# Moving crossbar transposes behind the weight loads: PE transposes for twelve units instead of eight, in a fused attention and MLP kernel

## The chip, the cores and the metric

The kernel runs on one core of a Trainium2 chip. A core has TensorE (PE: matrix products and transposes into PSUM), VectorE (DVE), ScalarE (ACT), GpSimd (POOL) and SyncE (SP, which here only issues transfers), and 16 DMA engines that all of them share. The metric is device time in microseconds of a whole execution, the median of several runs. Times within an execution come from the hardware profiler and count from its first instruction.

## What is computed

Attention with a feature map of exponentials, over 8 batches and 8 heads (576 rows, 64 columns each), and behind it, on the joined heads, a normalization and a two-layer MLP with a residual:

```python
def phi(x):
    proj = einsum('bhsd,df->bhsf', x, w_phi)              # 64 -> 128 features
    proj = proj - max(abs(proj), axis=-1, keepdims=True)
    return concatenate([exp(proj), exp(-proj)], axis=-1)
q_p, k_p = phi(q), phi(k)
kv  = einsum('bhsf,bhsd->bhfd', k_p, v)
z   = sum(k_p, axis=2)
num = einsum('bhsf,bhfd->bhsd', q_p, kv)
den = einsum('bhsf,bhf->bhs', q_p, z)[..., None] + 1e-06
x = (num / den).transpose(0, 2, 1, 3).reshape(8, 576, 512)
# ... then, row by row of x:
xn  = (x - mean(x)) / sqrt(var(x) + 1e-06) * g_ln
out = x + maximum(xn @ w_ch1, 0) @ w_ch2                  # 512 -> 2048 -> 512
```

Inputs and output are float32. Products run in bf16.

## The kernel before

**Units and pairs.** The 64 heads are worked on two at a time: 32 *units*, numbered n, of two heads each (rows of two heads side by side make 128 partitions' worth of columns). Eight units make a *pair* of batches (4 pairs). When a pair's units are done, its rows x are normalized, transposed (tile xT) and go through the MLP in three rounds of 384 rows: `hT_ps` = first product, `hT` = relu, `ch_ps` = second product, `o` = result, stored.

**Order of work.** All operations are given to a list scheduler that runs in Python when the kernel is built. Each has a rank, guessed durations and dependencies; the scheduler plays them through and puts them into each engine's program in the order in which its model started them. The ranks are latest start times plus an offset per kind of operation (table `OFF`, one row for each of three stages of the kernel), found by tuning. Engines then run their programs strictly in order.

**q and k must be turned.** The feature product needs q and k with their 64 columns on the partitions. There are two ways. For units below QK_DMA, PE turns the upper halves of the float32 words (bf16 by truncation), 8 transposes for the rows in the main tiles and 1 for the mixed tile that holds the last rows, and VectorE or ScalarE copies them out of PSUM:

```python
X_DMA, QK_DMA = 1, 8
# ...
def a_trans(u):
    # ... main: into PSUM tile qkT_ps (8 transposes)
    nc.tensor.transpose(
        ps[:, (i * 4 + c) * P : (i * 4 + c + 1) * P],
        qkb[:, i, hh, 4 * c * D + 1 : 4 * (c + 1) * D : 2], ident,
    )
    # ... mixed: into PSUM tile qxT_ps (1 transpose)
    # then copies into u["qkT"]: ("DVE", "ACT"), modelled (0.6, 0.93) and (0.16, 0.22) us
```

For the rest, the tile is first cast to bf16 (on whichever of VectorE, ScalarE and GpSimd the scheduler picks), and one transfer on SyncE's queue turns all nine 128x128 tiles through the crossbar on its way from SBUF to SBUF:

```python
def a_trans_dma(u):
    # ... cast_mixed, cast_main: ("DVE", "ACT", "POOL")
    def turn():
        u["qkT"] = qkT_bufs[j]
        nc.sync.dma_start_transpose(
            out=u["qkT"].rearrange("p (c t) -> p c t", t=P), in_=b16
        )
    dma("SP", rank, 0, turn, r=[("b16x", n % 2), ("b16", n % 2)],
        w=[("qxT", j), ("qkT", j, 0), ...], us=1.2, tiles=72)
```

In pair 0 the PSUM tile of the main transposes comes from the small tiles' pool (`ps_B`, three buffers); from unit 8 on it would come from `ps_A`, two large buffers that the scores of k and q (`pm`), the tails (`pt`) and the numerators (`num`) use as well.

**After the turn**, per unit: `pm` = scores of k and of q (4 products each), their maxima on VectorE (`m`), exponentials on ScalarE (`eb`, and `ea` from `pt`), scaled v on GpSimd (`vv`), `KV` on PE and a copy, numerators `num` on PE, their scaling on VectorE (`numc`, `rden`), and the division into x on GpSimd.

**Weights.** w_phi is loaded twice, into both halves of the partitions, and cast into a block-diagonal `wbk`. g (`gln`) scales the normalized rows. w_ch1 and w_ch2 (4.2 MB each in float32) are cast on the way by GpSimd's queue in four pieces each:

```python
nc.scalar.dma_start(out=wphi_f[0:D, :], in_=w_phi)
nc.scalar.dma_start(out=wphi_f[D : 2 * D, :], in_=w_phi)
# ... casts into wbk on VectorE
def load_w1(n, V, gate):      # waits for an early q/k/v load to have come
def load_w2(n, V):            # four loads, after the last piece of w1 has come
    # ...
    dma("POOL", V, 1 << 20, emit, r=[("w1 came", NW - 1)], w=[("w2", n)], us=0.85)
```

**The filler.** Until the scheduler's time 45 (WARM), PE gets a product of zeros whenever it has nothing else, so that it doesn't fall idle (line L1215, 120 columns each).

**The first loads**, by queue:

```python
load_main("k", 0, 1, -4.0, "SP")
load_main("q", 0, 1, -4.0, "ACT")
load_tails("k", 0, -3.0, "SP")
load_tails("q", 0, -3.0, "ACT")
load_main("v", 0, 1, -2.8, "SP")
load_main("k", 1, 1, -2.6, "SP")
load_main("q", 1, 1, -2.6, "ACT")
load_tails("v", 0, -2.4, "SP")
load_weights()                # g, on ACT's queue
load_main("v", 1, 1, -1.0, "SP")
```

Of the kernel before, what the change touches and what calls it, by code (L numbers as in the profile page):

```python
# [17 lines left out]
def bcast(ap: bass.AP, dim: int, n: int) -> bass.AP:  # L18
# [2 lines left out]
    return dataclasses.replace(ap, ap=new_ap)  # L21


DUE = 24.7
BLOCK = 127.5
RELU = -983.1
WARM = 45.0
X_DMA, QK_DMA = 1, 8
GATE = (("k", 3), ("k", 3), ("v", 3), ("v", 3))
OFF = (  # L30
    {
        "load": 291.2, "trans": 434.7, "trans.copy": 59.4, "mixed": -235.7, "mixed.max": -33.4,
        "mixed.exp": 269.7, "k": -70.1, "k.max": 134.5, "k.em": -242.4, "k.exp": -244.7,
        "en": 2.0, "vv": -236.4, "q": 197.1, "q.max": 56.3, "q.em": 267.7, "tails": -434.9,
        "tails.exp": -54.1, "kv": -342.1, "kv.copy": 60.1, "num0": -115.0, "num1": -4.8,
        "num.dve": 25.8, "put": 44.8, "ln": 232.4, "w1": -144.2, "w2": 330.3,
    },
    {
        "load": -33.4, "trans": 205.3, "trans.copy": 224.5, "mixed": 13.2, "mixed.max": -126.5,
        "mixed.exp": -37.8, "k": -79.5, "k.max": 229.0, "k.em": -204.8, "k.exp": 170.4,  # L40
        "en": -210.7, "vv": 14.0, "q": 271.6, "q.max": 83.8, "q.em": -232.1, "tails": -412.8,
        "tails.exp": -43.8, "kv": 80.5, "kv.copy": 400.8, "num0": -204.4, "num1": -95.2,
        "num.dve": 30.7, "put": 84.9, "ln": 271.1, "w1": -341.2, "w2": -67.5,
    },
    {
        "load": 108.9, "trans": 8.9, "trans.copy": 96.2, "mixed": -247.8, "mixed.max": -231.2,
        "mixed.exp": 118.7, "k": -33.5, "k.max": 47.1, "k.em": 39.2, "k.exp": 9.3, "en": -174.0,
        "vv": -109.4, "q": -27.3, "q.max": 37.9, "q.em": 195.5, "tails": -210.6,
        "tails.exp": 417.3, "kv": 29.7, "kv.copy": 177.5, "num0": 79.5, "num1": 83.1,
        "num.dve": -26.3, "put": -25.4, "ln": 1.0, "w1": -277.0, "w2": 28.2,  # L50
    },
)

# [131 lines left out]
def kernel(  # L185
# [21 lines left out]
    nc = tc.nc  # L207
    P = 128

    B, H, S, D = q.shape  # L210
# [3 lines left out]
    KC = DM // P  # L214
# [7 lines left out]
    TG = 4  # L222
# [6 lines left out]
    NM = RN // P  # L229
    XB = 3  # L230
    QB = 3
    NW = 4
# [13 lines left out]


    wphi_f = consts.tile([P, F], FP32, name="wphi_f")
    nc.scalar.dma_start(out=wphi_f[0:D, :], in_=w_phi)
    nc.scalar.dma_start(out=wphi_f[D : 2 * D, :], in_=w_phi)  # L250
    gln_sb = consts.tile([P, KC], FP32, name="gln")
    ngln = consts.tile([P, KC], FP32, name="ngln")
# [58 lines left out]
    add = sched.add  # L311
# [4 lines left out]

    backlog = {"DMA": 0.0, "DMA_w": 0.0}

    def dma(queue, rank, nbytes, emit, r=(), w=(), us=0.6, lag=2.2, tiles=0, row=1024):


        key = ("dma", len(sched.ops))
        kind, other = ("DMA_w", "DMA") if queue == "POOL" else ("DMA", "DMA_w")
        ns = 0.094 if queue == "POOL" else 0.018 if row == 256 else 0.046
        packets = nbytes / (2048 if queue == "POOL" else row) / 16
        pieces = max(1, round(packets * ns / 1.2))

        def transfer(now, free):
            backlog[kind] -= packets / pieces
            if tiles:  # L330
                return tiles * 0.015
            both = free.get(other, 0.0) > now
            turn = 0.046 if queue == "POOL" else 0.094
            return packets * (ns + turn * both) / pieces

        def issued(now, free):
            both = free.get(other, 0.0) > now or backlog[other] > 0
            wait = max(0.0, free.get(kind, 0.0) - now) + backlog[kind] * (0.046 + 0.094 * both)
            backlog[kind] += packets
            return max(us, wait) if tiles else us  # L340


        add(queue, issued, rank, emit, r=r, w=(key, *w))
        for i in range(pieces):
            last = i == pieces - 1
            add(kind, transfer, rank, None, r=(key, *r) if last else (key,),
                w=(*w, key) if last else (key,), lag=lag if last else 0.0)

    def issue(queue, rank, dst, src, keys, nbytes, row=1024):
        eng = nc.sync if queue == "SP" else nc.scalar  # L350
        dma(queue, rank, nbytes, lambda: eng.dma_start(out=dst, in_=src), w=keys, row=row)

    def heads(pair, i, half):

# [36 lines left out]
    def load_tails(key, n, rank, queue):  # L391

        t = {"q": q, "k": k, "v": v}[key]
        pair, i = divmod(n, H)
        j = n // TG % 2
        for half in range(2):
            b, h, step = heads(pair, i, half)
            ps_ = slice(half * 64, half * 64 + 64)
            dst = vx_bufs[j][ps_, :, half, 0:D] if key == "v" else (
                qx_bufs[j][ps_, :, "qk".index(key), :]  # L400
            )
            src = bass.AP(
                tensor=t.tensor, offset=t.offset + ((b * H + h) * S + 4 * P) * D,
                ap=[[D, 64], [step * S * D, TG], [1, D]],
            )
            issue(queue, rank, dst, src, [(key + "x" + str(half), j)], 16384 * TG, row=256)

    def loaded(u, key):
        g, hh, j = u["g"], u["hh"], u["n"] // TG % 2
# [1 line left out]

    def load_weights():
        def gln():
            nc.scalar.dma_start(out=gln_sb, in_=moe_g_ln.rearrange("(kc p) -> p kc", p=P))

        dma("ACT", -1.5, 2048, gln, w=["gln"])
        add(
            "DVE", 0.1, (0.0,), lambda: nc.vector.tensor_scalar_mul(out=ngln, in0=gln_sb, scalar1=-1.0),
            r=["gln"], w=["ngln"],
        )  # L420
# [108 lines left out]
    def a_trans_dma(u):  # L529

        n = u["n"]
        j = n % QB
        b16 = b16_bufs[n % 2]

        def cast(engine, out, in_):
            if engine == "DVE":
                nc.vector.tensor_copy(out=out, in_=in_)
            elif engine == "ACT":
                nc.scalar.copy(out=out, in_=in_)
            else:  # L540
                nc.gpsimd.tensor_tensor(
                    out=out, in0=in_, op=ALU.mult,
                    in1=bcast(bcast(one[:, 0], 1, in_.shape[1]), 2, in_.shape[2]),
                )

        def cast_mixed(engine):
            cast(
                engine, b16[:, MX * P :].rearrange("p (i d) -> p i d", i=2),
                qx_bufs[n // TG % 2][:, n % TG, :, :],
            )  # L550

        def cast_main(engine):
            cast(
                engine, b16[:, 0 : MX * P].rearrange("p (i f) -> p i f", i=2),
                qk_bufs[u["g"] % NBUF][:, :, u["hh"], :],
# [8 lines that stand above are left out]
        rank = rk("trans", n)  # L564
        add(("DVE", "ACT", "POOL"), (0.12, 0.22, 0.4), rank, cast_mixed, r=[*loaded(u, "q"), *loaded(u, "k")],
            w=[("b16x", n % 2)])
        add(("DVE", "ACT", "POOL"), (0.6, 1.02, 2.1), rank, cast_main, r=[*loaded(u, "q"), *loaded(u, "k")],
            w=[("b16", n % 2)])
        dma("SP", rank, 0, turn, r=[("b16x", n % 2), ("b16", n % 2)],
            w=[("qxT", j), ("qkT", j, 0), ("qkT", j, 1), *[("T", j, i) for i in range(3)]], us=1.2, tiles=72)  # L570

    def a_mixed(u):

# [342 lines left out]
    def x_trans_dma(pr, r, V):  # L916
        xi, j = (pr["pair"] * NR + r) % len(xc_bufs), (pr["pair"] * NR + r) % XB

        def turn():
            nc.sync.dma_start_transpose(  # L920
                out=xT_bufs[j], in_=xc_bufs[xi].rearrange("p i f -> p (i f)")
            )

        dma("SP", V, 0, turn, r=[("xc", xi, i) for i in range(NM)],
            w=[("xT", j, kc) for kc in range(KC)], us=1.2, tiles=NM * KC * 8)

    def x_stats(pr, t, half, V):

# [169 lines left out]
    for pair in range(NPAIR):  # L1098
# [5 lines left out]
        for i in range(H):  # L1104
            n = pair * H + i
# [12 lines left out]

    moe_V = 1000.0
    add("POOL", 5.0, -9.0, None)  # L1120
    add("ACT", 1.8, -9.0, None)
    add("SP", 0.7, -9.0, None)
    add("DVE", 4.3, -9.0, None)
    add(
        "ACT", 1.3, -1.0,
        lambda: nc.scalar.preload_act_table_set("natural_log_exp_and_others"),
# [4 lines left out]
    load_tails("q", 0, -3.0, "ACT")  # L1131
    load_main("v", 0, 1, -2.8, "SP")
    load_main("k", 1, 1, -2.6, "SP")
    load_main("q", 1, 1, -2.6, "ACT")
    load_tails("v", 0, -2.4, "SP")
    load_weights()
    load_main("v", 1, 1, -1.0, "SP")
# [5 lines left out]
    for n in range(NU + 2):  # L1143
        m = n + 4
        if n % HG == 0 and m < NU:
            rank = rk("load", m)
# [31 lines left out]
        if n >= 1 and n <= NU:  # L1178
            w = units[n - 1]
            pr, i = pairs[w["pair"]], w["i"]  # L1180
            V = rk("ln", n - 1)
            tiles = range(NT)
            if w["pair"] == 0:
                tiles = range(4) if i < 4 else range(4, NT)
                half, i = i % 4 // 2 if i % 2 else None, i % 4 + 4 * (i == 7)
            else:
                half = i // 4 if i % 4 == 3 else None
# [65 lines left out]
```

## Time and profile before

| what | value |
|---|---|
| time, median of 3 runs | 390.57 us (389.93 to 390.85) |
| span of the profiled run | 388.8 us, mean granted PE clock 0.988 |
| packets and bytes | 92444 packets, 53.28 MB, mean 137 GB/s |
| crossbar transposes of q and k | 24 (units 8 to 31), median landing 3.2 to 5.3 us by tile |
| filler products | 22.4 us of PE's busy time |
| MLP first product, second product | 153.3 us and 145.3 us of PE's busy time |

The lines of the profile itself stand in the prediction, where each is read. A few things on reading them. In the page's 40 slices one slice is 9.72 us here; a digit is tenths of busy time, and on the clock's row tenths of full speed. In a timeline a row is a run of like instructions: start, duration, engine, line of the kernel, operation, output<-input, count, and in brackets how long the engine was idle before it and what ended that. SPq, ACTq and POOLq are sequencers that issue transfers; a transfer's end isn't in that row but in the answer's "DMA to landing". Products on PE are pipelined: a single row's duration includes the way through the array, so the pace of a group is its total over its count.

### The profile page before, as it was taken

How to read it: one execution, taken by the hardware profiler on the slowest of the kernel's cores; microseconds unless marked ns; L12 is line 12 of the kernel's file. 1: busy time of each engine (PE TensorE's matmuls, PEld its weight loads, DVE VectorE, ACT ScalarE, POOL GpSimd, SP SyncE). 2: the span in 40 equal slices, each digit the busy share in tenths (PEclk: the TensorE clock that was granted, in tenths of full speed). 3: DMA queues.
4: the chain of work that ended last, by engine and by line, in shares of the span. 5: the costliest groups of instructions: out<-in, count | busy, mean ns of one | idle time of the engine just before them, and what ended most of it. 6: DMA issues, size and time to landing. Idle time of an engine off the chain costs nothing.

```text
span 388.8 us, 8917 instructions
## 1 busy us (share of the span) xinstructions
PE 364.6 (94%) x3307; PEld 232.5 (60%) x3354; DVE 255.0 (66%) x556; ACT 259.8 (67%) x576; POOL 201.9 (52%) x348
## 2 busy tenths in 40 slices
PE   3999995999999989999999999999999999999993
PEld 1888864666766554666666556666665555555541
DVE  3788995899999999997897998696757000000000
ACT  2877885899786857797976887686946444444411
POOL 3667987577576836664936655935841111111022
PEclk9999998799999999999999999999999999999998
DMA  7999889979799284948861486220007030110012
GB/s 208 300 227 279 262 150 170 222 189 254 197 245 232 64 230 111 236 129 190 183 186 36 124 163 157 57 60 2 30 27 137 31 90 29 27 56 27 30 66 71
DMA packets 92444, 53.28 MB, mean 137 GB/s; under 512 B 58992, under 2 KB 87792, under 8 KB 92400
## 3 DMA queue, kind: packets, MB, share of 16 engines
q1 hardware_dynamic: 86400, 47.79, 48.8%
q0 software_dynamic: 4224, 4.19, 6.9%
q10 hardware_dynamic: 1776, 0.72, 0.7%
q8 instruction: 26, 0.43, 0.5%
q14 instruction: 18, 0.15, 0.1%
HBM read 36.77 MB, written 9.44 MB: 119 GB/s over the span
## 4 chain that ended last, share of the span: by engine, by line
PE 57%; issue 21%; DVE 11%; DMA 6%; POOL 3%; ACT 1%; POOLq 0%; SPq 0%; DVEq 0%
PE hT_ps L1006 20%; PE ch_ps L1037 16%; PE pm L624 6%; DMA qkT_130<-b_0_131 4%; PE n_bank L734 3%; POOL o L1056 3%; PE num L780 3%; PE n_bank L1215 2%; PE pt L699 2%; DVE m_137 L631 1%; DVE m_135 L631 1%; DMA qx_106<-in_k_dram 1%; DVE w_120 L451 1%; DVE st_147 L933 1%; PE n_bank L729 1%
## 5 line engine op out<-in xcount | busy, mean ns | idle before, releaser
L1037 PE MATMUL ch_ps<-w_121,hT 128*128 128x512 bf16 x541 | 145.3, 379 | 1.6
L1006 PEld LDWEIGHTS <-w_120 128*128 128x128 bf16 x768 | 72.7, 98 | 55.9 <-issue 2.5
L1016 ACT ACTIVATE hT<-hT_ps 128x384 bf16<-128x384 f32 x113 | 55.6, 493 | 59.4 <-PE hT_ps L1006 58.9
L1037 PEld LDWEIGHTS <-hT 128*128 128x128 bf16 x576 | 53.3, 98 | 43.8
L820 POOL TENSOR_TENSOR x<-numc,rden 128x384 bf16<-128x384 f32 (+3 forms) x88 | 46.2, 541 | 62.4 <-DVE rden L814 58.2
L1056 POOL TENSOR_TENSOR o<-o,x 128x512 f32<-128x512 f32 x26 | 30.1, 1157 | 85.9 <-ACT o L1050 80.5
L1006 PE MATMUL hT_ps<-xT_127,w_120 128*128 128x384 bf16 x256 | 52.0, 326 | 0.1
L1006 PE MATMUL hT_ps<-xT_125,w_120 128*128 128x384 bf16 x256 | 50.2, 329 | 1.4 <-DVE hT L1014 0.9
L1006 PE MATMUL hT_ps<-xT_126,w_120 128*128 128x384 bf16 x256 | 51.2, 326 | 0.1
L1014 DVE TENSOR_SCALAR hT<-hT_ps 128x384 bf16<-128x384 f32 x79 | 42.9, 549 | 9.8 <-PE hT_ps L1006 9.2
L643 ACT ACTIVATE eb_134<-pm 128x1024 bf16<-128x1024 f32 x32 | 32.8, 1036 | 3.5 <-DVE m_137 L631 1.5
L643 ACT ACTIVATE eb_133<-pm 128x1024 bf16<-128x1024 f32 x32 | 31.7, 1025 | 4.9 <-DVE m_137 L631 3.8
L705 ACT ACTIVATE ea_118<-pt 128x1024 bf16<-128x1024 f32 x32 | 31.9, 1032 | 4.0 <-PE pt L699 2.4
L705 ACT ACTIVATE ea_116<-pt 128x1024 bf16<-128x1024 f32 x32 | 31.5, 1028 | 4.2 <-PE num L786 1.5
L631 DVE TENSOR_REDUCE m_136<-pm 128x8 f32<-128x1024 f32 x22 | 26.6, 1215 | 6.4 <-PE pm L624 6.3
L631 DVE TENSOR_REDUCE m_135<-pm 128x8 f32<-128x1024 f32 x22 | 26.7, 1215 | 4.0 <-PE pm L624 4.0
L1045 DVE SCALAR_TENSOR_TENSOR o<-ch_ps,rstd_157,x 128x512 f32<-128x512 f32 x2 | 1.5, 752 | 41.4 <-PE ch_ps L1037 41.4
L631 DVE TENSOR_REDUCE m_137<-pm 128x8 f32<-128x1024 f32 x20 | 24.3, 1214 | 2.1 <-PE pm L624 2.1
L1215 PE MATMUL n_bank<-wz 128*128 128x120 bf16 x301 | 22.4, 221 | 1.6 <-DVE KV L742 1.0
L804 DVE TENSOR_TENSOR numc<-num,em 128x390 f32<-128x390 f32 (+1 forms) x40 | 20.3, 515 | 4.6 <-PE num L780 4.4
L810 DVE TENSOR_TENSOR numc<-numc,num 128x390 f32<-128x390 f32 (+1 forms) x40 | 20.4, 515 | 0.7
L1215 PEld LDWEIGHTS <-wz 128*128 128x128 bf16 x301 | 18.6, 101 | 3.1 <-issue 2.1
(204 smaller groups left out, 649.5 us busy)
## 6 DMA issues: line engine op xcount, KB each, us to landing
out_dram<-o SPq DMA_DIRECT2D x32, 256.0 KB, 2.5
qk_100<-in_k_dram SPq DMA_DIRECT2D x12, 256.0 KB, 3.8
v_101<-in_v_dram SPq DMA_DIRECT2D x12, 256.0 KB, 3.7
qk_102<-in_k_dram SPq DMA_DIRECT2D x10, 256.0 KB, 3.4
qk_102<-in_q_dram SPq DMA_DIRECT2D x10, 256.0 KB, 4.1
v_103<-in_v_dram SPq DMA_DIRECT2D x10, 256.0 KB, 4.6
qk_104<-in_k_dram SPq DMA_DIRECT2D x10, 256.0 KB, 4.0
qk_104<-in_q_dram SPq DMA_DIRECT2D x10, 256.0 KB, 4.7
```

What stands on the lines that cost most here:

```text
L624: nc.tensor.matmul(ps[:, 2 * c : 2 * c + 2, :], u["qkT"][:, (i * 4 + c) * P : (i * 4 + c + 1) * P], wbk, start=True, stop=True,)
L631: nc.vector.reduce_max(out=u["m"][:, i, 0:MX], in_=u["pm", i], axis=AX.X, apply_absolute_value=True)
L643: nc.scalar.activation(u["EB"][:, t, 0:MX, :], u["pm", 1], AF.Exp, scale=(1.0, -1.0)[t])
L705: nc.scalar.activation(u["EA"][:, t, 0:1024], u["pt"], AF.Exp, scale=(1.0, -1.0)[t])
L810: nc.vector.tensor_add(out=st["numc"], in0=st["numc"], in1=st["ps"][0])
L820: nc.gpsimd.tensor_tensor(out=dst, in0=st["numc"][ps_, i : i + n, 0:D], in1=bcast(st["rden"][ps_, i : i + n], 2, D), op=ALU.mult,)
L1006: nc.tensor.matmul(st["ps"], w1_sb[:, kc, jj * P : (jj + 1) * P], xT_bufs[(pair * NR + r) % XB][:, kc::KC, :], start=(kc == 0), stop=(kc = ...
L1014: nc.vector.tensor_relu(h_sb, st["ps"])
L1016: nc.scalar.activation(h_sb, st["ps"], AF.Relu)
L1037: nc.tensor.matmul(ch[t], hT[r, jj][:, rt * P : (rt + 1) * P], w2_sb[:, jj, :], start=(jj == 0), stop=(jj == JC - 1),)
L1056: nc.gpsimd.tensor_tensor(out=ch["o", t], in0=ch["o", t], in1=x[:, t, :], op=ALU.add)
L1215: nc.tensor.matmul(warm, wz, wz[:, 0:WN], start=False, stop=False, skip_group_check=True)
```

## The change

It has five parts.

- QK_DMA goes from 8 to 12: units 8 to 11, the first half of pair 1, are turned on PE instead of through the crossbar.
- The first crossbar transpose, now that of unit 12, waits for all four pieces of w_ch2.
- The two halves of w_phi go out on two queues, SyncE's and ScalarE's, instead of both on ScalarE's.
- The second unit's q and g move from ScalarE's queue to SyncE's.
- The scheduler's model of transfers changes (issue 0.5 us and landing 1.5 us instead of 0.6 and 2.2; a transpose keeps its queue for 1.29 us; the start of each engine is set anew), and the whole table of offsets is tuned again. This changes the order of work everywhere.

It is meant to keep crossbar transposes apart from the loads of the weights, and to start the first products sooner.

```diff
-DUE = 24.7
-BLOCK = 127.5
+DUE = 39.9
+BLOCK = 136.7
-X_DMA, QK_DMA = 1, 8
+X_DMA, QK_DMA = 1, 12
 OFF = (
     {
-        ... "ln": 232.4, "w1": -144.2, "w2": 330.3,
+        ... "ln": 323.9, "w1": -204.9, "w2": 513.0,
     },
     # ... (all entries of all three rows are new)
@@ w_phi
-    nc.scalar.dma_start(out=wphi_f[0:D, :], in_=w_phi)
+    nc.sync.dma_start(out=wphi_f[0:D, :], in_=w_phi)
     nc.scalar.dma_start(out=wphi_f[D : 2 * D, :], in_=w_phi)
@@ model of a transfer
-    def dma(queue, rank, nbytes, emit, r=(), w=(), us=0.6, lag=2.2, tiles=0, row=1024):
+    def dma(queue, rank, nbytes, emit, r=(), w=(), us=0.5, lag=1.5, tiles=0, row=1024):
-        pieces = max(1, round(packets * ns / 1.2))
+        pieces = 1 if tiles else max(1, round(packets * ns / 1.2))
             if tiles:
-                return tiles * 0.015
+                return 0.1
@@ g
-            nc.scalar.dma_start(out=gln_sb, in_=moe_g_ln.rearrange("(kc p) -> p kc", p=P))
-        dma("ACT", -1.5, 2048, gln, w=["gln"])
+            nc.sync.dma_start(out=gln_sb, in_=moe_g_ln.rearrange("(kc p) -> p kc", p=P))
+        dma("SP", 0.15, 2048, gln, w=["gln"])
@@ a_trans_dma
-        dma("SP", rank, 0, turn, r=[("b16x", n % 2), ("b16", n % 2)],
-            w=[("qxT", j), ("qkT", j, 0), ("qkT", j, 1), *[("T", j, i) for i in range(3)]], us=1.2, tiles=72)
+        dma("SP", rank, 0, turn, r=[("b16x", n % 2), ("b16", n % 2)]
+            + [("w2", i) for i in range(NW) if n == QK_DMA],
+            w=[("qxT", j), ("qkT", j, 0), ("qkT", j, 1), *[("T", j, i) for i in range(3)]], us=1.29, tiles=72)
@@ starts of the engines in the model, first loads
-    add("ACT", 1.8, -9.0, None)
-    add("SP", 0.7, -9.0, None)
-    add("DVE", 4.3, -9.0, None)
+    add("ACT", 1.3, -9.0, None)
+    add("SP", 1.3, -9.0, None)
+    add("DVE", 3.6, -9.0, None)
-    load_main("q", 1, 1, -2.6, "ACT")
+    load_main("q", 1, 1, -2.5, "SP")
```

## The prediction

> **What bounds the kernel now.** I first read the first two parts of the page, shares of engines and the span in 40 slices, because they say which engine could set the end and where it fails to.
>
> ```profile
> PE 364.6 (94%) x3307; PEld 232.5 (60%) x3354; DVE 255.0 (66%) x556; ACT 259.8 (67%) x576; POOL 201.9 (52%) x348
> PE   3999995999999989999999999999999999999993
> DVE  3788995899999999997897998696757000000000
> PEclk9999998799999999999999999999999999999998
> ```
>
> PE is busy 94% of the span. It has one dent in the middle (the 5 in the seventh slice, 58 to 68 us), and there its granted clock drops as well (8 and 7). But in the first 48 us "busy" isn't work: the kernel pads PE with products of zeros (the filler, L1215) to keep its clock. So I asked for busy time by stage: all instructions first, then those of L1215 alone, whose first row is the last line here. The columns are the stretch, its length, busy us and count of each engine, granted clock, DMA share, GB/s.
>
> ```profile
> 0.00:48.00 48.00, 39.52 (x613) 35.03 (x617) 35.43 (x83) 33.07 (x75) 31.32 (x74) 1.00 1.02 258
> 48.00:63.00 15.00, 14.00 (x179) 10.10 (x178) 14.03 (x30) 12.85 (x32) 12.92 (x24) 1.00 0.95 151
> 63.00:75.00 12.00, 7.79 (x63) 5.10 (x61) 6.85 (x16) 6.76 (x12) 6.05 (x15) 0.72 1.23 233
> 120.00:160.00 40.00, 37.52 (x305) 21.81 (x309) 38.72 (x85) 29.46 (x66) 25.42 (x37) 1.00 0.67 178
> 160.00:200.00 40.00, 39.68 (x397) 26.31 (x400) 35.17 (x70) 32.50 (x70) 24.09 (x41) 1.00 0.74 180
> ...
> 0.00:48.00 48.00, 22.18 (x299) 18.50 (x299) 1.00 1.02 258
> ```
>
> There are three regimes. **The head**, to 48 us: PE does 39.5 - 22.2 = 17.3 us of real work; VectorE, ScalarE and the transfers (share 1.02) set its pace. **The body**, from 48 us to the last product at about 382.5: there is no filler, and PE is the bound (39.68 of 40 us from 160 to 200). **The tail**, 6 us of last result, addition and store. In a body bound by PE each idle microsecond and each microsecond of slow clock moves the end one for one. From 120 to 160 PE idles 2.5 us, because VectorE is full (38.72 of 40). The other hole is 63 to 75, and the timeline shows whose it is (start, duration, engine, line; in brackets the idle time before and its releaser):
>
> ```profile
> 51.05 2.30 POOL L435 DMA_DIRECT2D w_121<-in_moe_w_ch_dram  x3
> 52.16 2.38 SPq L560 DMA_TRANSPOSE qkT_130<-b_0_131  x1
> 55.06 0.81 POOL L435 DMA_DIRECT2D w_121<-in_moe_w_ch_dram  x1
> 60.56 6.37 SPq L560 DMA_TRANSPOSE qkT_128<-b_1_132  x1
> 67.59 1.03 PE L624 MATMUL pm<-wbk,qkT_130 128*128 128x256 bf16 x4 [3.71 <-DMA qkT_130<-b_0_131]
> 67.76 0.69 DVE L537 CAST b_0_131<-qk_104 128x1024 bf16<-128x1024 f32 x1 [3.87 <-DMA qkT_130<-b_0_131]
> 67.62 0.30 ACT L539 CAST b_0_131<-qx_106 128x128 bf16<-128x128 f32 x1 [3.31 <-DMA qkT_130<-b_0_131]
> ```
>
> The first crossbar transpose (unit 8) is issued at 52.16, between the second weight matrix's loads (51.05 to 55.9), and lands at 67.54. PE, VectorE and ScalarE all end up waiting for it. The groups for its source and for the weight tile give the usual landing times, minimum, median and maximum:
>
> ```profile
> DMA to landing us min/median/max: 3.2/3.6/15.4
> DMA to landing us min/median/max: 8.8/13.6/15.9
> ```
>
> So the 15.4 us belong to one transpose, not to the operation: its median is 3.6, and 15.4 is the length of a weight load. The chain that ended last also runs through this transfer (4.0% of the span, its largest DMA share).
>
> **What the Trainium skill says.** "DMA: Bandwidth & Descriptors", section Issuing engines are not separate DMA queues, says that transfers of every issuing engine run on the same 16 DMA engines and interleave. The trace agrees: a transpose from SyncE was held up under loads from GpSimd. The same page (Rules for kernel authors) says a transpose beside ordinary transfers needs nothing. That is about correctness; in time the trace shows 15.4 against 3.6 us. "VectorE: DVE Perf Modes", section The three transpose paths, advises TensorE for a 128x128 transpose if the output may go to PSUM. In the trace eight such transposes on PE follow each other in 0.45 us, plus a copy out of PSUM. "TensorE: Matmul & The Clock Gate", section What's actually happening, says the clock is gated to half unless PE has been busy. Here the windows read 0.50 from 66 to 72 us, after the 3.7 us gap, and 0.93 from 72 to 74.
>
> **The change, part by part.**
>
> (1) *The stall goes.* With the first crossbar transpose moved from unit 8 to unit 12 and made to wait for the second weight matrix, none is under way beside those loads. In the body 24 units pass from 75 to about 300 us, where VectorE falls silent: 225 / 24 = 9.4 us each, so unit 12 is due some 4 x 9.4 = 38 us after unit 8: near 100 us, when the weights (last issued at 55.9, at most 15.9 to land) have long been in. What the stall costs, from the PE timeline between 63.88 and 75.12 us (11.24 us): 20 products hT at 0.1625 (3.25), 8 products pm at 0.109 (0.87), and about 0.85 for KV, tails, the mixed chunk and numerators, in all 5.0 us at full speed. Lost: 11.24 - 5.0 = **6.2 us**, namely 3.7 idle and about 2.5 of half clock. I credit all of it.
>
> (2) *PE transposes for units 8 to 11.* Each is 8 main and 1 mixed transpose. Eight take 0.45 us, so nine take 0.51; four units: **+2.0 us** on PE, in a stage where PE is the bound.
>
> (3) *Casts become copies.* The four casts that go were one on ScalarE (1.04), two on GpSimd (1.88 each) and one on VectorE (0.69), plus the mixed ones (0.2 to 0.3). The copies out of PSUM are 0.68 us on VectorE or 1.05 on ScalarE, mixed 0.21 or 0.27. GpSimd is relieved of 3.8 us; the other two take about 2 x 0.85 = 1.7 more. From 75 to 120 VectorE is busy 43.0 of 45 us and ScalarE 37.4, so ScalarE has 7.6 us of room, and it hides there. PSUM: these copies take one of the two large buffers for about 1.3 us per unit. The k scores hold one about 4 us, q 1.7, tails 2.5, numerators 1.6, so 10 of the 19 buffer-microseconds in a 9.4 us unit become 11. **0**, at worst +0.5.
>
> (4) *Head.* The two halves of w_phi are issued at 0.75 and 1.35 on ScalarE's queue, and their casts start at 3.78 and 4.85. The second holds back the copy of the first transposed k (5.10) behind it on VectorE, while its product had been there since about 4.1. With a half on each queue both can land near 3.8, but k of unit 0 goes out about 0.6 us later on SyncE's queue (landed 3.5, so about 4.1). The first copy can start near 4.6 instead of 5.1: **-0.5 us**. q of unit 0 and its tails go out 0.6 us earlier on ScalarE's queue; q1 and g leave that queue, which frees the table load (6.35). Whether this reaches 48 us depends on VectorE being the limit all the way; it is 84 to 100% busy from 20 us on. I keep -0.5.
>
> (5) *New order.* All ranks are redrawn, with transposes now modelled at 1.29 + 1.5 us instead of as short work on a DMA queue. No single row gives this a size. The candidates are the 2.5 us idle from 120 to 160 and 1.0 us idle from 48 to 63; attention reaching that stage some 4 us earlier should help. I take **-1.5**, a choice rather than a measurement, with 3 us either way.
>
> Sum: -6.2 + 2.0 + 0 - 0.5 - 1.5 = -6.2 us, so 390.57 - 6.2 = 384.4; call it **384.5 us**.
>
> **The rivals.**
>
> *A, the wait moves.* Transposes and loads leave SyncE in program order. A transpose that waits for weights holds every load behind it, and the new offset of the weights (513.0 against 330.3) may send them off later. For: SyncE already sat 6.37 us in one transpose. Against: the 38 us of slack in (1). If so, the hole of 63 to 75 returns elsewhere, shorter; about 388 to 391 with the extra PE work.
>
> *B, PE isn't the only bound.* VectorE and ScalarE lost nearly 4 us in the stall too, and if they set the pace from 48 to 160, removing it gives no more than their 3.5 us plus the clock, while the copies cost them. For: VectorE's 38.72 of 40. Against: from 160 on PE is 99% busy and VectorE at most 88%, so arrears are made up. About 387.
>
> *C, more than the stall.* With attention ahead, products of the MLP start earlier than 49 us and replace filler, or the idle from 120 to 160 vanishes. For: 22 us of filler. Against: the head is full on VectorE and the transfers, and its first product needs all of units 0 to 3. About 381.
>
> **Range and chances.** The spread comes from (5), about 3 us either way, and from A and B on one side and C on the other: 380.5 to 389.0. Two per cent faster means below 382.8, which needs C or a lucky order: 0.29. Slower than 398.4 would need a new stall as large as the old one and more: 0.03. The rest is 0.68.
>
> **What would show it.** (1) is right if no transpose lands more than about 6 us after issue, none starts before the second weight matrix has landed, and the clock stays at 1.00 from 50 to 350 us. (2): 96 main and 12 mixed transposes of q and k on PE (64 and 8 now), and PE's busy time without the filler (342.2 now) about unchanged: 2.0 us more work, 2.5 less of slow clock. (3): no new wait of PE for the copy of units 8 to 11. (4): the first pm products before 5.3 us instead of 5.58. (5): idle of PE from 75 to 300 below 3 us (4.1 now, by the same windows). The prediction is wrong if the first transpose sits on SyncE's queue with loads behind it, if the second product (ch_ps) waits for late weights, or if the first product of the MLP starts well away from 49 us: a later start is paid nearly one for one.

## The result, and the profile after

The changed kernel takes **394.54 us** (394.33 to 397.26), beside 390.31 us for the kernel before: a ratio of 1.0123, 95% interval 1.0077 to 1.0169. It is slower, by 4.2 us. The prediction said 384.5 us and a range of 380.5 to 389.0. It was wrong by 10.0 us and in direction.

First the same rows as before, from the first two parts of the page of the changed kernel:

```profile
PE 366.5 (93%) x3315; PEld 233.4 (60%) x3364; DVE 254.4 (65%) x553; ACT 262.1 (67%) x583; POOL 197.5 (50%) x343
PE   3999799999999999999999998999999999999993
PEclk9999989999999999999999999999999999999998
```

The dent of the seventh slice is gone, and with it the slow clock there. In its place stand a 7 in the fifth slice (39 to 49 us) with an 8 on the clock's row just after it, and an 8 in the twenty-fifth (235 to 245 us). Neither was there before. The table of stretches (length, busy us and count of PE, PEld, VectorE, ScalarE, GpSimd, then clock, DMA share, GB/s) gives them a size:

```profile
0.00:48.00 48.00, 37.15 (x569) 32.68 (x574) 35.38 (x79) 34.05 (x72) 33.05 (x80) 1.00 1.02 258
48.00:63.00 15.00, 14.79 (x169) 11.42 (x171) 13.92 (x28) 10.54 (x32) 8.62 (x17) 0.89 1.11 210
63.00:75.00 12.00, 11.14 (x117) 7.27 (x115) 11.82 (x31) 12.00 (x27) 9.37 (x25) 1.00 0.79 211
120.00:160.00 40.00, 38.97 (x330) 23.33 (x334) 37.96 (x85) 30.38 (x72) 24.36 (x37) 1.00 0.78 194
160.00:200.00 40.00, 39.36 (x374) 25.32 (x378) 31.23 (x64) 30.58 (x72) 27.36 (x44) 1.00 0.66 159
200.00:250.00 50.00, 46.94 (x413) 28.93 (x419) 41.37 (x88) 35.65 (x77) 22.54 (x38) 1.00 0.43 101
```

The last stretch in the kernel before:

```profile
200.00:250.00 50.00, 49.58 (x434) 30.65 (x441) 41.64 (x93) 39.36 (x92) 31.52 (x51) 1.00 0.49 112
```

From 63 to 75 PE is busy 11.14 of 12 us at full clock (7.79 at 0.72 before): the stall was removed as planned. From 120 to 160 it idles 1.0 us instead of 2.5. But in the head it idles 10.85 instead of 8.48, from 48 to 63 its clock is 0.89, and from 200 to 250 it idles 3.1 us where the same stretch of the kernel before had 0.4.

The timeline of SyncE's queue and the landing times of the transposes (minimum, median, maximum):

```profile
77.81 2.16 SPq L564 DMA_TRANSPOSE qkT<-b  x1
DMA to landing us min/median/max: 3.2/3.5/5.7
```

The first transpose is issued at 77.81, after the last piece of the second weight matrix has landed (67.6), and none takes over 5.7 us. The longest before was 15.4.

So the intended mechanism worked and the time still rose. The question was which new waits took the gain, and whether they belong to the moved transposes, the moved first loads or the new order.

### The profile page after: what moved, and what is told of

Read it like the earlier page. It is cut to its first block, busy times and chain, and to the rows that moved or that the text cites. A ratio compares the mean times of both kernels' runs of the same rounds, so it can differ in the third digit from the quotient of the medians.

```text
span 392.3 us, 8899 instructions
## 1 busy us (share of the span) xinstructions
PE 366.5 (93%) x3315; PEld 233.4 (60%) x3364; DVE 254.4 (65%) x553; ACT 262.1 (67%) x583; POOL 197.5 (50%) x343
## 4 chain that ended last, share of the span: by engine, by line
PE 50%; issue 23%; DVE 10%; ACT 6%; DMA 6%; POOL 4%; ACTq 1%; POOLq 0%; DVEq 0%
PE hT_ps L1012 16%; PE ch_ps L1043 12%; PE pm L630 6%; DMA qkT<-b 4%; PE n_bank L1221 4%; PE n_bank L740 3%; POOL o L1062 3%; PE num L786 3%; DVE m L637 2%; ACT ea L711 2%; PE pt L705 2%; DVE st L939 2%; DVE xc L957 1%; DMA qx<-in_q_dram 1%; PE qkT_ps L475 1%
## 5 line engine op out<-in xcount | busy, mean ns | idle before, releaser
L1012 PE MATMUL hT_ps<-xT,w 128*128 128x384 bf16 x768 | 153.4, 326 | 0.9 <-DVE numc L816 0.3
L1043 PE MATMUL ch_ps<-w,hT 128*128 128x512 bf16 x539 | 144.7, 379 | 1.6
L1012 PEld LDWEIGHTS <-w 128*128 128x128 bf16 x768 | 72.1, 98 | 56.0 <-issue 1.5
L637 DVE TENSOR_REDUCE m<-pm 128x8 f32<-128x1024 f32 x64 | 77.4, 1215 | 17.0 <-PE pm L630 16.9
L826 POOL TENSOR_TENSOR x<-numc,rden 128x192 bf16<-128x192 f32 (+3 forms) x88 | 46.1, 538 | 62.5 <-DVE rden L820 59.1
L649 ACT ACTIVATE eb<-pm 128x1024 bf16<-128x1024 f32 x64 | 64.3, 1029 | 14.9 <-DVE m L637 13.6
L711 ACT ACTIVATE ea<-pt 128x1024 bf16<-128x1024 f32 x64 | 63.7, 1042 | 6.0 <-PE pt L705 3.7
L663 POOL TENSOR_TENSOR vv<-v,em 128x512 bf16<-128x512 f32 x32 | 33.7, 1052 | 22.0 <-issue 8.5
L630 PE MATMUL pm<-wbk,qkT 128*128 128x256 bf16 x256 | 39.4, 282 | 3.2 <-DMA qkT<-b 2.1
L663 POOL TENSOR_TENSOR vv<-v,en 128x512 bf16<-128x512 f32 x32 | 33.9, 1059 | 1.1 <-ACT en L656 1.0
L1221 PE MATMUL n_bank<-wz 128*128 128x120 bf16 x275 | 20.8, 225 | 1.6 <-DVE KV L748 1.1
```

The costliest lines, as they stand in the source:

```text
L630: nc.tensor.matmul(ps[:, 2 * c : 2 * c + 2, :], u["qkT"][:, (i * 4 + c) * P : (i * 4 + c + 1) * P], wbk, start=True, stop=True,)
L637: nc.vector.reduce_max(out=u["m"][:, i, 0:MX], in_=u["pm", i], axis=AX.X, apply_absolute_value=True)
L649: nc.scalar.activation(u["EB"][:, t, 0:MX, :], u["pm", 1], AF.Exp, scale=(1.0, -1.0)[t])
L663: nc.gpsimd.tensor_tensor(out=u["vv"][:, t, 0:MX, 0:D], in0=vb[:, hh, :].rearrange("p (c d) -> p c d", d=D), in1=bcast(e[:, 0:MX], 2, D), ...
L711: nc.scalar.activation(u["EA"][:, t, 0:1024], u["pt"], AF.Exp, scale=(1.0, -1.0)[t])
L826: nc.gpsimd.tensor_tensor(out=dst, in0=st["numc"][ps_, i : i + n, 0:D], in1=bcast(st["rden"][ps_, i : i + n], 2, D), op=ALU.mult,)
```

## The experiments

Each kernel is compared with the kernel before on the same chip; the ratios and their 95% intervals leave disturbed executions out. My theory at the start was that the new order of work costs more than the stall did, through a late start of the MLP. The rivals were that twelve units on PE cost more PE time than they save, and that the moved first loads hurt.

### One part at a time

**Transposes only.** The kernel before, with QK_DMA = 12 and the wait for the weights; offsets, model and first loads stay.

```diff
-X_DMA, QK_DMA = 1, 8
+X_DMA, QK_DMA = 1, 12
+            + [("w2", i) for i in range(NW) if n == QK_DMA],
```

> The kernel before with one part of the change alone: units 8 to 11 are turned on PE and the first crossbar transpose waits for the second weight matrix. Offsets, the model of transfers and the first loads stay as before (the scheduler still redraws the order, because the operations differ). Theory 1, the moved transposes are a gain and the newly tuned order is the loss: 390.3 - 5.6 (stall, as the stages of the two traces show it) + 1.6 (transposes on PE) = 386.3 us, give or take 2 for the redraw. Theory 2, turning on PE and waiting for the weights is itself the loss: 393 to 395 us.

Measured: 392.47 us, ratio 1.0059 (1.0040 to 1.0078). The stretch from 63 to 75 is mended here too (9.91 us busy, clock 1.00), but from 48 to 63 PE falls from 14.00 to 12.00 us. There the MLP's first product waits 3.3 us in two pieces for VectorE's relu, where the kernel before waits 0.9 us. The longer piece, 1.9 us, stands behind a centring operation on VectorE (xc, explained below) that took 1.53 us instead of 0.34. The stretch from 63 to 75 gained 2.1 us of idle time and about 2.2 us of slow clock (an estimate, 7.79 x 0.28); this and more was given back elsewhere, and only the part from 48 to 63 was located.

**Order only.** The changed kernel with QK_DMA = 8 and without the wait for the weights.

> The changed kernel with that part undone: crossbar transposes from unit 8 on, no wait for the weights; new offsets, new model, new first loads are kept. Theory 1: the stall at the weight loads comes back on top of an order that costs as much as before, 394.5 + 4.3 - 1.6 = 397 us, give or take 2. Theory 2: the loss goes with the part, 389 to 391 us.

Measured: 410.32 us, ratio 1.0513 (1.0480 to 1.0547). The first transpose, issued at 54.63, lands at 66.92, so the stall's cause is back. It isn't all: the first three centring operations take 5.66 us here, and PE is busy only 32.67 of 40 us from 160 to 200. Since any edit of the list of work makes the scheduler draw a new order, "one part alone" is never quite that, and the next runs asked how much a redraw does by itself.

**First loads only**, in two ways: once with the scheduler redrawing, once with the order of before kept instruction by instruction while only the queues of four transfers change.

```diff
-    nc.scalar.dma_start(out=wphi_f[0:D, :], in_=w_phi)
+    nc.sync.dma_start(out=wphi_f[0:D, :], in_=w_phi)
-    load_main("q", 1, 1, -2.6, "ACT")
+    load_main("q", 1, 1, -2.5, "SP")    # and g; in the second kernel the model still books both on ACT
```

> The kernel before with another part of the change alone: w_phi's halves on two queues, the second unit's q and g on SyncE's queue, with the model's start times that go with it; offsets and the rest as before. Theory 1 (the newly tuned offsets and the model's times of transfers are the loss): 389.8 us, between 388.5 and 391.5, with the first scores on PE near 5.1 us instead of 5.58. Rival (the moved loads delay the first units): above 392 us, with units 1 to 3 later than before.

> The kernel before with the moved first loads (w_phi's halves on two queues, the second unit's q and g on SyncE's queue), but in exactly the order of before on PE, VectorE and GpSimd: only the queues of these four transfers differ. If the 7.9 us that the first loads cost in the earlier run came from the redrawn order, this is 389 to 391 us. If the moved loads themselves delay the first units, it is 394 to 398 us.

Measured: 398.19 us (1.0206, 1.0177 to 1.0236) redrawn, and 391.23 us (1.0038, 1.0013 to 1.0064) in the old order. In the second the first pm product starts at 5.37 instead of 5.58 and the MLP's first product at 48.12 instead of 49.13. That microsecond brings nothing, as the first transpose still lands at 67.49, under the weights; and it may not come from the moved loads, since executions with the same first loads and the same order up to there reach the first centring anywhere from 42.79 to 44.05 us. The moved loads are not what made the kernel slow: in the old order they cost 0.4%, about 1.5 us, and the redraw is worth another 7 us.

### How much a redraw alone is worth

These five kernels do the same work as the kernels that they are drawn from. One constant of the scheduler's model of a product (its fixed part, in ns) is moved by 0.2, and the order comes out different.

```diff
-        return n * (cols / 2.4 + 4.0) / 1000.0
+        return n * (cols / 2.4 + 4.2) / 1000.0    # or 3.8
```

> The kernel before, with nothing changed but one constant of the scheduler's model: a product on PE is modelled 0.2 ns longer (4.2 for 4.0). The program does the same work; only the order is drawn again. Theory R, the order of before is a picked one and a redraw with the same offsets costs several microseconds: 393 to 399 us. Rival, the order matters little: 389.5 to 391.5 us.

> The kernel with the moved transposes alone (12 units on PE, first crossbar transpose behind the weights, old offsets), drawn again by the same constant (4.2 for 4.0). Theory R with a real gain of the moved transposes: 389 to 394 us, some 4 us under the redrawn kernel before. If the moved transposes gain nothing by themselves: the same as the redrawn kernel before, within 1.5 us.

> The changed kernel, order drawn again by the same constant (4.2 for 4.0). If its new offsets are tuned to its order as well as the old ones were to theirs, a redraw costs 2 to 6 us: 396 to 400 us. If the new offsets' order is no better than a draw at random: 391 to 396 us.

> The kernel before drawn again a second time, with the constant at 3.8 instead of 4.0. From the first redraw (402.7) and the run with the first loads (398.2, a redraw as well): 396 to 404 us if redraws of before cost 8 to 12 us; 390 to 392 us if the first redraw was bad luck.

> The kernel with the moved transposes alone, drawn again a second time (3.8). If the moved transposes save 4 to 5 us on average over draws: 392 to 398 us, below the second redraw of before. If they save nothing: equal to it within 1.5 us.

| kernel | as tuned (4.0) | 4.2 | 3.8 |
|---|---|---|---|
| before | 390.3 | 402.70 (1.0314, 1.0272 to 1.0356) | 392.88 (1.0068, 1.0042 to 1.0093) |
| before with transposes moved | 392.47 | 397.27 (1.0181, 1.0139 to 1.0222) | 393.11 (1.0062, 1.0044 to 1.0081) |
| after | 394.54 | 399.75 (1.0231, 1.0167 to 1.0294) | not run |

The same work spreads over 12 us. Both tuned orders are better than the redraws by this constant (a redraw of the changed kernel by another constant, further down, came out at 392.60). Read down the columns, moving the transposes is worth +2.2, -5.4 and +0.2 us: its gain by itself can't be separated in this way. Only kernels with the same order can be compared to a microsecond, and so the rest of the study edits the changed kernel within its own order.

### The late start of the MLP

Timeline rows for VectorE and GpSimd (start, duration, engine, line, operation, output<-input, count), the first of the kernel before, the others of the changed kernel:

```profile
44.21 1.66 DVE L951 TENSOR_SCALAR xc_123<-x,mv_144 128x512 bf16<-128x512 bf16 x3
43.71 4.37 DVE L957 TENSOR_SCALAR xc<-x,mv 128x512 bf16<-128x512 bf16 x3
44.21 1.04 POOL L663 TENSOR_TENSOR vv<-v,en 128x512 bf16<-128x512 f32 x1
...
46.84 0.40 POOL L672 TENSOR_TENSOR vv<-vx,en 128x130 bf16<-128x130 f32 x1
47.18 3.04 POOL L439 DMA_DIRECT2D w<-in_moe_w_ch_dram  x4
```

VectorE's three centring operations xc subtract the mean from the first rows and are the last step ahead of the MLP's transposes. They should take 0.34 us each. In the changed kernel the first one takes 3.68 us (0.99 in the kernel before). It ends at 47.39, just after GpSimd's row of scalings vv, eight instructions without a gap, has ended at 47.24 and GpSimd has turned to issuing transfers. PE runs dry and its clock falls (stretches of 2 us, columns as above):

```profile
46.00:48.00 2.00, 0.46 (x2) 0.19 (x2) 2.00 (x3) 0.00 (x0) 2.00 (x5) 1.00 1.05 250
48.00:50.00 2.00, 1.86 (x19) 1.67 (x20) 2.00 (x5) 1.19 (x4) 2.00 (x3) 0.63 0.82 102
50.00:52.00 2.00, 2.00 (x20) 1.67 (x19) 1.74 (x3) 0.58 (x1) 0.23 (x1) 0.51 1.10 172
```

The MLP's first product starts at 52.04 (49.13 before), and part of what PE does until then runs at half clock.

"SBUF — State Buffer" of the Trainium skill (section SBUF: two separate sides) says that VectorE and GpSimd share a pair of ports as an exclusive lock: for VectorE operations in a two-port fast mode, or with two SBUF inputs, the one that starts first holds it for its whole instruction and the other blocks. The trace agrees in so far as VectorE is late beside GpSimd, but the wait here spans a whole row of GpSimd instructions. Three runs test whether GpSimd is the cause.

**Centring on ScalarE.** Same order; the three operations of the first round go to ScalarE.

```diff
-            if engine == "DVE":
+            if engine == "DVE" and not (pair == 0 and t < NM):
```

> The changed kernel, same order on PE, with one thing else: the centring of the first three row tiles (xc, round 0 of pair 0) runs on ScalarE instead of VectorE, in the same place of the order. In the changed trace one of these three took 3.68 us instead of 0.33, beside an unbroken row of GpSimd operations from 43.70 to 47.2 us. Theory of the shared memory port: PE starts the MLP some 3 us sooner and the time falls to 391.5 us (391 to 392.5). Rival, the late start has another cause (transfers, first units late) and the slow centring only fills a wait: 394 to 394.7 us.

Measured: 394.11 us, ratio 1.0102 (1.0053 to 1.0152). Inconclusive: ScalarE did them only from 48.2 to 51.0, behind its own queue, and in the profiled execution the last rows of q of the first batch of units landed at 23.1 instead of 18.1 us, so that the head was late before this point.

**Centring with a stride.** The same three operations walk each row with a stride of two elements; values and order stay. The idea was that this form leaves the fast mode, and so shouldn't block if the lock is taken for that mode only.

```diff
+                if pair == 0 and t < NM:
+                    o_, x_ = (a.rearrange("p (a b) -> p b a", b=2) for a in (o_, x_))
```

> The changed kernel, same order on every engine, with one thing else: the centring of the first three row tiles on VectorE walks its bf16 elements with a stride of two instead of in a row. If the 3.7 us of one of these operations came from a memory port that VectorE's fast mode shares with GpSimd, the strided form runs at about 0.6 us each, beside GpSimd's operations; PE starts the MLP about 2 us sooner, and the time falls by 1.5 to 2.5 us, to about 392.5. If it came from something else (late data, the order), the three stay as long and the time stays at 394.5 us.

Measured: 395.23 us, ratio 1.0115 (1.0085 to 1.0144): no gain. The timeline has

```profile
44.05 4.92 DVE L960 TENSOR_SCALAR xc<-x,mv 128x512 bf16<-128x512 bf16 x3
```

and the first of the three takes 3.84 us: this form blocks as well. It doesn't decide about the fast mode, since no run shows that the form leaves it: the third of the three takes 0.49 us, where 0.6 was expected of the slower mode, and 0.51 in the changed kernel without a stride.

**GpSimd waits.** Rather than freeing VectorE's operation, GpSimd is held back: before its scalings of unit 4 it reads eight elements of the third centred tile, which it can do only when that tile is written.

```diff
         def scale_main(t):
+            if n == 4 and t == 0:
+                nc.gpsimd.tensor_copy(out=seen, in_=xc_bufs[0][:, NM - 1, 0:8])
```

> The changed kernel, same order, three buffers as it has them, with GpSimd's wait for the centring alone. If the two costs are apart, it falls from 394.5 by the 3.9 us that the same edit gave on top of the fourth buffer, to 390.6 us (390 to 391.5). If the gain needed the fourth buffer: 392 to 394.5 us.

Measured: 389.66 us, ratio 0.9996 (0.9972 to 1.0020). Two rows of its timeline:

```profile
42.79 1.22 DVE L960 TENSOR_SCALAR xc<-x,mv 128x512 bf16<-128x512 bf16 x3
46.41 0.81 PE L1015 MATMUL hT_ps<-xT,w 128*128 128x384 bf16 x4
```

This alone is 4.9 us less than the changed kernel, whose own interval is 1.8 us to either side; on top of the fourth buffer (below) the same edit gives 3.9. Of the 5.6 us by which the MLP starts sooner, 0.9 were there before the centring began (42.79 against 43.71). The cause of the late centring is shown: it is GpSimd's row that holds VectorE, whatever the exact rule of the lock. The read wasn't tried in the kernel before, whose three operations took 1.66 us instead of 1.22.

### The third qkT buffer

The chain of waits of the changed kernel (start, length, what) shows the second new cost:

```profile
240.12 0.43 PE pt L705 x2
240.58 4.91 DMA qkT<-b
245.54 0.61 PE pm L630 x4
```

A transpose into one of three qkT buffers can start only when the tails' product pt, which reads the tile that lay in that buffer before (three units back), is done at 240.55. It takes 4.91 us to land, and PE waits for it: 1.33 us here, 0.75 us at 201.4. The scheduler's model gives a transpose 1.29 + 0.1 + 1.5 = 2.9 us since the change (1.2 + 1.08 + 2.2 = 4.5 before), and the trace 3.2 to 5.7. It plans the consumer earlier than the tile can come. A held-up transpose keeps its source tile too: the casts that refill it wait 7.4 us in all on VectorE and 5.0 on ScalarE.

**A fourth buffer.** Same order, one more qkT tile in rotation:

```diff
-    qkT_bufs = [... for i in range(QB)]
+    qkT_bufs = [... for i in range(QB + 1)]
-            u["qkT"] = qkT_bufs[j]
+            u["qkT"] = qkT_bufs[n % (QB + 1)]
```

> The changed kernel, same order on every engine, with a fourth buffer for the turned q and k. In the changed trace several crossbar transposes after 190 us start only when the tails' product three units before has read their buffer, and PE then waits for them (0.75 us at 201, 1.33 us at 245). Theory, the new order packs reader, transpose and next product closer than a transpose's 3.2 to 4.9 us, and the buffer passes it on: idle time of PE from 160 to 300 us falls by 1.5 to 3 us, to about 392.5 us in all. Rival, PE there waits for VectorE and ScalarE anyway: 394 to 394.8 us.

Measured: 390.90 us, ratio 1.0011 (0.9991 to 1.0032): 3.6 us less than the changed kernel. The stretch from 200 to 250:

```profile
200.00:250.00 50.00, 49.60 (x432) 30.23 (x428) 43.64 (x92) 37.58 (x87) 24.32 (x42) 1.00 0.46 110
```

PE's idle time there falls from 3.1 to 0.4 us, and the casts' waits fall to 1.2 and 0.6 us.

The counter-test gives the same buffer to the kernel before and to the one with the transposes moved, both drawn with the old model:

> The kernel before, same order on every engine, with a fourth buffer for the turned q and k. If the wait for that buffer is a cost of the new order, before gains nothing: 389.8 to 390.8 us. If any order pays it, before falls by 2 us or more, to 388.5 or below.

> The moved transposes alone with the old offsets (392.5 us), same order, with the fourth buffer. If an order that wasn't tuned for the moved transposes pays for that buffer too: 389.5 to 391.5 us. If the wait belongs to the new offsets alone: 392 to 393 us.

Measured: 389.72 us (0.9992, 0.9973 to 1.0011) and 393.08 us (1.0081, 1.0050 to 1.0111; it was 392.47). Neither gains. The wait belongs to the new order, not to moving the transposes.

**The model's landing time.** The changed kernel, redrawn with a transpose landing 3.1 us after its issue in the model instead of 1.5:

```diff
-lag=lag if last else 0.0)
+lag=(3.1 if tiles else lag) if last else 0.0)
```

> The changed kernel with three buffers, but the scheduler's model lets a transpose land 3.1 us after its issue instead of 1.5 (4.5 us in all instead of 2.9; the traces show 3.2 to 5.7). The order is redrawn by it, which alone costs some microseconds either way. If the short model packs the users of a transpose too close, the waits of PE's two queues for qkT fall from 7.7 us in sum to below 3, whatever the total: 392 to 399 us. If the model has no part in it, they stay at 5 us or more.

Measured: 392.60 us, ratio 1.0064 (1.0046 to 1.0081). In the waits of the two kernels (total us, times, longest), two lines of the changed kernel and then one of this run:

```profile
PEld L630 <- DMA qkT<-b: 3.5, 6, 1.6
PE pm L630 <- DMA qkT<-b: 2.1, 2, 1.3
PEld L630 <- DMA qkT<-b: 0.3, 1, 0.3
```

PE's waits for transposes go from 5.6 to 0.3 us, counted on both of its queues, weight loads (PEld) and products, which overlap. (The 7.7 us of the expectation holds 2.1 us more, for ScalarE's copies of tiles turned on PE; these stay at 2.0.) The centring operations are still blocked in this order (4.37 us for three, first MLP product at 50.03), so the gain is 1.9 us only; and being a redraw it carries that scatter too. The waits are the firm part of it.

### Together

**Fourth buffer and GpSimd's wait:**

> The changed kernel with the fourth qkT buffer, same order, and one thing more: GpSimd reads eight elements of the third centred tile before it starts the scaled v of unit 4, so it waits there until the centring is done instead of the other way round. If the centring stands behind GpSimd's row of operations, it ends near 45.5 instead of 47.5 us, the first product of the MLP starts near 50 instead of 51.6 us, and the time falls from 390.9 to 389 us (388.3 to 389.8). If the start of the MLP has another limit, GpSimd is only later: 390.5 to 392 us.

Measured: **386.98 us**, ratio 0.9917 (0.9889 to 0.9944). The timeline of VectorE, GpSimd and PE, one row of each:

```profile
43.86 1.22 DVE L960 TENSOR_SCALAR xc<-x,mv 128x512 bf16<-128x512 bf16 x3
45.14 0.19 POOL L661 COPY seen<-xc 128x8 bf16<-128x8 bf16 x1 [0.74 <-DVE xc L960]
47.47 0.81 PE L1015 MATMUL hT_ps<-xT,w 128*128 128x384 bf16 x4
```

The three centrings take 1.22 us, GpSimd pays 0.74 us of waiting and a read of 0.19, and the MLP starts at 47.47.

**The casts as well.** VectorE is late in the same way at the casts ahead of the first crossbar transpose: the main cast on VectorE takes 1.64 us and the mixed one 1.58, where 0.69 and 0.22 are usual. This kernel adds two more such reads, ahead of the scalings of units 8 and 9, each of the casts' tile.

```diff
+            if n in (8, 9) and t == 0:
+                c0 = (n - 8) * MX * P
+                nc.gpsimd.tensor_copy(out=seen, in_=b16_bufs[0][:, c0 : c0 + 8])
```

> The best kernel so far (fourth buffer, GpSimd waits for the centring: 387.0 us) with two more waits of the same kind: GpSimd reads eight elements of each of the two casts for unit 12 before the scaled v of units 8 and 9. These casts took 1.63 and 1.58 us at 70 us instead of 0.66 and 0.22, and PE then idled 1.4 us. If PE's idle there is theirs: 385.7 to 386.7 us. If another wait takes its place: 386.7 to 387.5 us.

Measured: **385.66 us** (384.30 to 385.78), ratio 0.9871 (0.9840 to 0.9901): faster than both kernels. The mixed cast in the timeline, of the changed kernel and of this one; then the next eight main transposes of a unit on PE, of the kernel without the two new reads and of this one; then this one's stretch from 63 to 75:

```profile
76.16 1.58 DVE L541 CAST b<-qx 128x128 bf16<-128x128 f32 x1
70.77 0.22 DVE L542 CAST b<-qx 128x128 bf16<-128x128 f32 x1
74.42 0.61 PE L476 MATMUL qkT_ps<-ident,qk 128*128 128x128 bf16 x8 [1.01 <-DVE m L638]
73.30 0.61 PE L476 MATMUL qkT_ps<-ident,qk 128*128 128x128 bf16 x8
63.00:75.00 12.00, 11.51 (x115) 7.30 (x113) 11.35 (x29) 11.30 (x27) 10.77 (x28) 1.00 0.99 271
```

The crossbar transpose itself leaves no sooner (73.86, and 73.87 without the new reads). What comes sooner is the maximum m that VectorE takes after the casts: it frees a large PSUM buffer that PE had waited 1.0 us for.

## Why the prediction was wrong, step by step

**Step (1), the stall, was right.** No transpose starts before the weights have landed, the longest landing is 5.7 us (the prediction said about 6), and the hole of 63 to 75 is closed: 3.35 us less idle time and about 2.2 us of slow clock (an estimate, 7.79 x 0.28), some 5.5 of the 6.2 us predicted. Two readings of the step were off without harm. It took the long landing for one transpose's, but the next one, issued at 60.56, took 11.40 us as well. And it expected unit 12 near 100 us; its transpose left at 77.81, so the slack behind the weights was 10 us. The further sign, a clock of 1.00 from 50 us on, failed, but for the late MLP (0.51 from 50 to 52), not for a transpose.

**Step (2), twelve units on PE,** has the counts predicted, 96 main and 12 mixed transposes. PE's busy time without the filler is 345.7 us (366.5 - 20.8) instead of an unchanged 342.2. Part of the 3.5 us is work run at half clock from 48 to 52, and some product records are missing in both traces (541 and 539 of 576 second products are there). By group, the main transposes grew from 5.9 to 8.4 us and the mixed ones from 1.9 to 2.8, 3.4 us in all with each row's way through the array counted, so the term can be put at 2.0 to 3.4 us and no closer. (The advice of "VectorE: DVE Perf Modes" of the Trainium skill to turn a 128x128 tile on TensorE stands in its section Rules for kernel authors; the section that the prediction names has the times of the paths.)

**Step (3), copies for casts,** was right at 0. From 48 to 100 us PE's products wait for no copy of a turned tile. They wait once, for 1.0 us at 78.92, to put a transpose into a large PSUM buffer whose scores VectorE's maximum hadn't read yet; but this goes with the late casts, as the last experiment shows, and not with the copies.

**Step (4), the head,** did not show: the first pm products start at 5.60, not before 5.3. In the old order the moved loads brought it from 5.58 to 5.37, so a part of the 0.5 us may exist, but the new order doesn't use it.

**Step (5), the new order, is the step that failed.** It stood as -1.5 us, "a choice rather than a measurement, with 3 us either way". In its place the runs showed two waits that this order makes, worth 4.9 and 3.6 us each when one alone is removed and 7.6 us together (394.54 to 386.98), and a third of 1.3 us at the casts. These 8.9 us are nearly all of the 10.0 us of error. The sign for it failed too: idle time of PE from 75 to 300 is 6.85 us, where below 3 was predicted (1.85 with the three waits removed). The spread of 3 us was too small as well: redraws of the same work spread over 12 us.

The text had named the sign that came true, a first MLP product well away from 49 us and paid for nearly one for one. It named no cause for it, though, and none of the rivals has it: A (a moved wait on SyncE) did not happen, and B made VectorE too busy, while it was blocked with no more work than before (254.4 us against 255.0).

With the three waits of the order taken out, the change is worth -4.5 us (385.66 against 390.14 in the same runs). Steps (1) to (4) sum to -6.2 + 2.0 + 0 - 0.5 = -4.7. That the two agree so closely is partly luck: the -0.5 of step (4) did not show, the 2.0 may be 3.4, and GpSimd's reads were not given to the kernel before, which has slow casts and centrings too (up to 1.63 and 1.24 us).

**Open.** What moving the transposes is worth by itself isn't settled, since each redraw brings its own waits. Nor is the rule of the blocking: in the kernel before, the same operation got in after one long GpSimd instruction (0.99 us instead of 0.34), and in the changed one only after eight. Why the one row lets VectorE in and the other doesn't was not tried.

## What to carry to other kernels

When a change redraws a scheduled order, the new order is a term of its own with the spread of redraws, which can be measured by moving a model constant that should not matter; here it was larger than the effect studied. Before crediting a removed wait, check what the scheduler's model says of the operations put in its place against the trace (here 2.9 us for what takes 3.2 to 5.7), and whether there are buffers enough for the longer time. Where VectorE's short operation is late with all its inputs there, look at what GpSimd runs at that time: a read of a few elements that makes GpSimd wait was worth 4 to 5 us here.

## What the hardware showed that was not expected

- A VectorE operation of 0.34 us (bf16, 128x512, one scalar per row) took 3.68 us under an unbroken row of GpSimd operations and ended with that row. With a stride of two it took 3.84. Making GpSimd wait for it, by a read of 0.19 us, gave 3.9 to 4.9 us of the whole time.
- A transpose issued among the weight loads lands about when they do: at 66.3 to 68.3 us in each of seven kernels that issued it between 51 and 55 us (the kernel before, its two redraws, the same with a fourth buffer, the moved loads in both orders, and the order-only run). The third of the four pieces landed at 64.1 to 67.4 us in these. The usual time of a transpose is 3.5 us after issue.
- A crossbar transpose of nine tiles holds its queue for 1.3 us and lands 3.2 to 5.7 us after issue in the changed kernel, which has no weight loads beside it. That the queue is free again after 1.3 us says nothing of when PE can read the tile.
